# A two-dimensional Fourier mix and a gated expert: the Nyquist column broadcast by way of DRAM, and rows of x, fills and spills issued one transfer at a time

## The chip, the cores and the metric

The kernel runs on one core of a Trainium2 chip. The metric is the device time of one execution in microseconds. A core has five engines with programs of their own: TensorE (PE in the profile, its weight loads PEld), VectorE (DVE), ScalarE (ACT), GpSimd (POOL) and SyncE (SP), which here issues nearly all DMA transfers. All transfers of the core are carried by the same 16 DMA engines.

## The reference

All in float32. x has 8 batches of 3008 rows of 256 columns; w_in is 256 x 2048, w_out 2048 x 256.

```python
X = np.fft.fft(x, axis=1)          # over the 3008 rows
X = np.fft.fft(X, axis=2).real     # over the 256 columns
h = X.reshape(24064, 256) @ w_in
g = h * (1.0 / (1.0 + np.exp(-1.702 * h)))
out = g @ w_out
```

## The kernel before

**The transform.** 3008 is 47 x 64. Rows are viewed as 47 groups of 64; `fold1` and `mix1` do the length-47 part with matrices in `w1` on the tile `xt` (slots folded in pairs on POOL, then matmuls, then ACT copies back into `xt`). `spill` writes `xt` to the DRAM tensor `Td[b]`, `fill` reads it back in another layout into the tile `t4`, `rotate` corrects one column of it with a small matmul, and `stage2` does the length-64 part for a third of the rows, transposing the results on VectorE into the tile `pq`. Before a batch can be folded, `turn` writes the rows of x in reversed order into the DRAM tensor `Xr[b]` (three transfers), and `load_x` loads the forward and reversed rows into `xt` (four pieces of two transfers).

**The columns.** The transform over the 256 columns is folded into the weights: `wcs` holds w_in multiplied by cosines and sines. Since a real transform is symmetric, only half of the columns is stored; column 128 (the Nyquist column) takes the place of an unused part and is one row, partition 0 of `pq[:, 1]`, of 512 values. `nyquist` makes a tile `nb` of it in which all 128 partitions hold that row. ScalarE's `middle` (L566) multiplies `nb` by one factor a partition and writes the product into the PSUM bank x, to which the matmuls of `begin` (L495) then add the rest of the hidden layer.

**The expert.** The main loop goes over steps `(b, blk, hh, p)`: 8 batches, 3 blocks of `pq` a batch, 2 halves, 8 pairs of 128 hidden units: 384 steps. A step makes the hidden values of one pair for 2 x 256 outputs: sigmoid-gated forward values (L578) and, by the symmetry, backward values (L539, L581). From step 8 on the second product uses a Strassen-like scheme: `sums` and `deeper` form sums and differences on POOL and VectorE (L588 to L625), and the matmuls of `product` (L495) and `small_products` (L659) use seven products for eight, some of them twice nested. Products of step t run with step t + 3. At the end of each group of eight steps the result is combined, transposed into the tile `os` and stored by `store` (L799), in groups of four transfers.

**The order.** No scheduler reorders anything: the instructions of each engine stand in the order in which the Python code emits them. Work other than the steps' own hangs on slots: `at(t, fn, ...)` appends a function to slot t, and it is emitted at the end of step t. For batch b with t0 = 48 b, slots t0 + 6 on hold the folds and mixes of batch b + 1, then its spill, fill and rotate, and the turn and load of batch b + 2; slots t0 + 8, t0 + 24 and t0 + 40 hold the `stage2` of the next block, the slots after these its `nyquist`. In the first batch folds to loads come five slots later (`late`) and rotate three. A slot orders instructions on each engine and sets no time: an engine runs on until a semaphore holds it. SyncE's transfers take eight completion semaphores in turn, so an issue also waits for the transfer eight before it. `nb` and `pq` have two buffers, `xt` and `t4` one.

The very first block's `nyquist` is made by a matmul with a row of ones instead, and batch 0 is loaded and mixed by functions of its own ahead of the loop; neither is touched.

Of the kernel before, what the change touches and what calls it, by code (L numbers as in the profile page):

```python
# [27 lines left out]
F32 = mybir.dt.float32  # L28
# [6 lines left out]
NA, NB = 47, 64  # L35
NJ = NB // 2
NM = 48
ENDS = 0, NJ, NJ + 1, NJ + 2
PIECES = (0, 32), (32, NA)
# [7 lines left out]
def view(ap, offset, *dims):  # L47
    return bass.AP(ap.tensor, ap.offset + offset, [list(d) for d in dims])


def free(ap, offset, *dims):
    return bass.AP(ap.tensor, ap.offset + offset, [list(ap.ap[0])] + [list(d) for d in dims])
# [59 lines left out]
def kernel(ctx: ExitStack, tc, x, w_in, w_out, tab1, tab2, out):  # L112
    nc = tc.nc
    B, S, D = x.shape
    DF = w_in.shape[1]
    H = D // 2
    NF = DF // 128
    NBLK = NG // 4
# [10 lines left out]
    ctx.enter_context(tc.manual_schedule())  # L129

    Xr = [nc.dram_tensor(f"Xr{b}", (NA, NJ, D), F32, kind="Internal").ap() for b in range(B)]
    Td = [nc.dram_tensor(f"Td{b}", (NG * 128, D), F32, kind="Internal").ap() for b in range(B)]

    w1 = const.tile([128, (NJ + 3) * NM + 64 - NM], F32, tag="w1", name="w1")
# [31 lines left out]
    def bank(name, tag=None):  # L166
        if tag is None:
            tag = spare.pop(0)
            spare.append(tag)
        if tag in ("o0", "o1"):  # L170
            return o_banks[int(tag[1])]
        return (rest if tag[0] == "o" else psp).tile([128, 512], F32, tag=tag, name=name)
# [5 lines left out]
    t4t, pqt, nbt = {}, {}, {}  # L178
    xt = xp.tile([128, NJ, D], F32, tag="x", name="xt")

    def turn(b):

        for m0, m1 in ((NJ + 1, NJ + 17), (NJ + 17, NB)):
            n = m1 - m0
            nc.sync.dma_start(out=view(Xr[b], (m0 - NJ - 1) * D, [D, n], [NJ * D, NA], [1, D]),
                              in_=view(x[b], ((NA - 1) * NB + m0) * D, [D, n], [-NB * D, NA], [1, D]))
        nc.sync.dma_start(out=Xr[b][:, NJ - 1, :], in_=x[b].rearrange("(p j) d -> p j d", j=NB)[:, NJ, :])

    def load_x(b):

        for r in range(2):
            for p0, p1 in PIECES:
                t, src = xt[64 * r + p0:64 * r + p1], x[b].rearrange("(p j) d -> p j d", j=NB)[p0:p1]
                pairs = [4 * D, 8], [1, 2 * D]
                for lo, rows_, at in ((0, src, 2 * r), (16, Xr[b][p0:p1], 2 - 2 * r)):
                    nc.sync.dma_start(out=t[:, lo:lo + 16, :].rearrange("p (i c) d -> p i (c d)", c=2),
                                      in_=free(rows_, at * D, *pairs))

    e0 = {}

# [115 lines left out]
        for _ in range(n):  # L316
            nc.tensor.matmul(ps[:], lhsT=wcs[0][:, 0:128], rhs=wcs[0][:, 0:512], start=True, stop=True)

    def spill(b):

        for c in range(2):
            nc.sync.dma_start(out=view(Td[b], 16 * c * D, [NJ * D, NM], [1, 16 * D]),
                              in_=xt[64 * c:64 * c + NM, 0:16, :].rearrange("p q d -> p (q d)"))

    def fill(b, a0=0, a1=NG):
        if a0 == 0:
# [30 lines left out]
    def nyquist(b, blk):  # L357

        nb = nbt[b, blk] = pqp.tile([128, 512], F32, tag="nb", name="nb")
        row = pqt[b, blk][0:1, 1, :]  # L360
        if (b, blk) != (0, 0):
            nc.sync.dma_start(out=nb[:], in_=free(row, 0, [0, 128], [1, 512]))
            return
        ps = bank("psn")
        nc.tensor.matmul(ps[:], lhsT=ones[:], rhs=row, start=True, stop=True)
        nc.scalar.copy(nb[:], ps[:])


    raw = {}

# [457 lines left out]
    for e in odds:  # L828
# [7 lines left out]
                      in_=view(tab1, 0, [tab1.shape[1], 128], [28 * NM, 2], [1, ends]))  # L836
# [70 lines left out]
    def at(t, fn, *args):  # L907
        extra.setdefault(t, []).append((fn, args))

    n = len(steps)  # L910
# [9 lines left out]
        at(t, load_out, c, nc.sync)  # L920
    at(3, load_matrices)
    if B > 1:
        at(3, turn, 1)
        at(3, load_x, 1)
    at(4, rotate, 0, 4, NG)
    for i in range(NCK):
        at(7 + i, differences, i)
# [1 line left out]
    for b in range(B):  # L929
        t0 = b * NBLK * NF  # L930
        late = 0 if b else 5
        if b + 2 < B:
            at(t0 + 10, turn, b + 2)
        if b + 1 < B:
            for c in range(NCH):
                for part in range(2):
                    at(t0 + 6 + 2 * c + part + late, fold1, b + 1, c, part, nc.gpsimd)
                if c % 2:
                    at(t0 + 9 + 2 * c + late, mix1, b + 1, c // 2)
            at(t0 + 24 + late, spill, b + 1)  # L940
            at(t0 + 29 + late, fill, b + 1)
            if b + 2 < B:
                at(t0 + 33 + late, load_x, b + 2)
            at(t0 + 36 + 3 * (late > 0), rotate, b + 1)
        for blk in range(NBLK):
            nxt = (b, blk + 1) if blk + 1 < NBLK else (b + 1, 0)
            if nxt[0] < B:
                at(t0 + blk * NF + 8, stage2, *nxt)
                at(t0 + blk * NF + 9, nyquist, *nxt)

    for t in range(n + LAG):
        if t < NP:
# [7 lines left out]
            if t == 0:  # L960
                low_up(in2)
                nyquist(0, 0)
                low_down(in2)
# [94 lines left out]
```

## Time and profile before

| | us |
|---|---|
| median of 5 runs (lowest, highest) | 1876.4 (1874.68, 1877.94) |
| the profiled execution, device time | 1875.33 |
| its span in the profile | 1873.3 |
| ACT busy, L566 alone | 1149.7, 352.8 |
| SyncE's waits at L799 for the transposes into os | 1256.2 |
| issue of an nb broadcast on SyncE (median of 23) | 0.545 |
| DMA: bytes moved, mean rate | 105.21 MB, 56 GB/s |

The span is the time from the first to the last instruction in one profiled execution; the device time of that execution holds some 2 us more. Busy time is the time in which an engine had an instruction under way; issuing a transfer is not counted as busy. In a row of waits stand the engine and line that waited, what released it, and the total in us, the number of times and the longest. "Issue" as the releaser means that the engine waited for nothing that the profile shows.

### The profile page before, as it was taken

What the parts mean: (1) busy time and instruction counts of PE and PEld (TensorE: products, weight loads), DVE (VectorE), ACT (ScalarE), POOL (GpSimd) and SP (SyncE); (2) the same over time, 40 slices, a digit from 0 to 9 for tenths busy, and PEclk for the clock granted to TensorE, in tenths of its full rate; (3) what the DMA queues carried; (4) which work ended last, traced back from release to release, by engine and by line L of the source; (5) the groups of instructions that cost most, each with busy time, mean ns of one, the idle gap of its engine ahead of it and who ended that gap; (6) DMA issues with size and microseconds to landing.
All of it is one profiled execution on the core that took longest, in us unless ns stands there. A gap on an engine that the chain in (4) does not pass through costs nothing.

```text
span 1873.3 us, 55597 instructions
## 1 busy us (share of the span) xinstructions
PE 1851.7 (99%) x23600; PEld 1413.3 (75%) x23600; DVE 1532.1 (82%) x2245; ACT 1149.7 (61%) x2248; POOL 964.2 (51%) x1058
## 2 busy tenths in 40 slices
PE   9999999999999999999999999999999999999998
PEld 6577778777777777777777777777778777778776
DVE  7788878888789877988788878888788888878874
ACT  6655655666566656666565666656666656656663
POOL 4577345744367443673347733485435754434442
PEclk9999999999999999999999999999999999999999
DMA  8732351336221362305513164042631231312211
GB/s 283 172 52 17 80 90 19 51 51 118 24 18 47 53 121 19 52 17 97 77 15 52 23 117 53 13 63 46 111 25 25 19 51 47 29 15 17 20 22 23
DMA packets 145415, 105.21 MB, mean 56 GB/s; under 512 B 104914, under 2 KB 127986, under 8 KB 143984
## 3 DMA queue, kind: packets, MB, share of 16 engines
q1 hardware_dynamic: 143952, 101.14, 32.6%
q8 instruction: 186, 3.05, 0.7%
q10 hardware_dynamic: 1216, 0.52, 0.1%
q14 instruction: 61, 0.50, 0.1%
HBM read 58.38 MB, written 48.01 MB: 57 GB/s over the span
## 4 chain that ended last, share of the span: by engine, by line
PE 89%; DVE 5%; ACT 3%; DMA 1%; issue 1%; POOL 1%; SPq 0%; DVEq 0%; ACTq 0%; POOLq 0%
PE x L495 33%; PE o L495 25%; PE low L659 23%; PE o L659 4%; DVE big L625 2%; PE ps L348 1%; PE ps L246 1%; DVE big L762 1%; DVE big L539 1%; ACT x L566 1%; DMA big<-in_moe_w_in_dram 1%; PE psw L461 1%; ACT xt L249 1%; ACT big L581 0%; DVE big L671 0%
## 5 line engine op out<-in xcount | busy, mean ns | idle before, releaser
L596 POOL TENSOR_TENSOR big<-big 128x256 f32<-128x256 f32 (+1 forms) x376 | 349.9, 931 | 846.1 <-ACT big L588 716.3
L495 PE MATMUL x<-pq,wcs 128*64 128x256 f32 (+1 forms) x6016 | 777.6, 377 | 6.1 <-ACT x L566 3.1
L625 DVE TENSOR_TENSOR big<-big 128x512 f32<-128x512 f32 (+1 forms) x736 | 640.8, 885 | 30.8 <-PE low L659 14.3
L495 PE MATMUL o<-big,wo 128*64 128x256 f32 (+1 forms) x4800 | 627.1, 375 | 0.4 <-DVE big L603 0.4
L495 PEld LDWEIGHTS x<-pq,wcs 128*64 128x64 f32 x6016 | 415.6, 137 | 195.3 <-issue 14.6
L495 PEld LDWEIGHTS o<-big,wo 128*64 128x64 f32 x4800 | 345.5, 137 | 147.6 <-DVE big L603 1.2
L578 ACT ACTIVATE g<-x 128x512 f32<-128x512 f32 (+1 forms) x376 | 221.8, 590 | 374.9 <-PE x L495 373.8
L539 DVE TENSOR_TENSOR big<-g,x 128x512 f32<-128x512 f32 (+2 forms) x440 | 254.2, 589 | 202.8 <-ACT big L581 202.2
L659 PE MATMUL low<-big 128*64 128x128 f32 (+1 forms) x5888 | 385.1, 270 | 1.4 <-issue 1.4
L659 PEld LDWEIGHTS low<-big 128*64 128x64 f32 x5888 | 340.3, 137 | 29.7 <-issue 1.6
L566 ACT ACTIVATE x<-nb,af 128x256 f32<-128x256 f32 (+1 forms) x752 | 352.8, 469 | 12.2
L597 POOL TENSOR_TENSOR big<-big 128x256 f32<-128x256 f32 (+1 forms) x376 | 359.0, 955 | 0.0
L581 ACT ACTIVATE big<-x 128x512 f32<-128x512 f32 (+1 forms) x376 | 220.5, 586 | 201.3 <-PE x L495 185.4
L588 ACT ACTIVATE big<-big 128x512 f32<-128x512 f32 (+1 forms) x376 | 231.8, 616 | 44.9 <-DVE big L539 43.6
L659 PE MATMUL low<-big,wo 128*64 128x128 f32 (+1 forms) x2944 | 223.3, 271 | 0.1
L659 PEld LDWEIGHTS low<-big,wo 128*64 128x64 f32 x2944 | 174.9, 137 | 3.6 <-DVE big L625 0.4
L604 DVE TENSOR_TENSOR big<-big 128x512 f32<-128x512 f32 (+1 forms) x188 | 149.6, 796 | 6.5
L603 DVE TENSOR_TENSOR big<-big 128x512 f32<-128x512 f32 (+1 forms) x188 | 137.3, 730 | 4.7 <-POOL big L596 4.7
L659 PEld LDWEIGHTS o<-big,wo 128*64 128x64 f32 x1472 | 94.0, 137 | 24.6 <-issue 0.2
L762 DVE TENSOR_TENSOR big<-big,low 128x512 f32<-128x512 f32 (+3 forms) x184 | 109.1, 610 | 3.5
L659 PE MATMUL o<-big,wo 128*64 128x128 f32 (+1 forms) x1472 | 111.8, 271 | 0.0
L218 POOL TENSOR_TENSOR xt<-xt 111x510 f32<-111x510 f32 x56 | 77.2, 1379 | 4.4
(103 smaller groups left out, 975.2 us busy)
## 6 DMA issues: line engine op xcount, KB each, us to landing
out_dram<-os SPq DMA_DIRECT2D x284, 64.0 KB
Td<-xt SPq DMA_DIRECT2D x14, 768.0 KB
t<-Td SPq DMA_DIRECT2D x7, 1536.0 KB
xt<-in_x_dram SPq DMA_DIRECT2D x14, 512.0 KB
xt<-Xr SPq DMA_DIRECT2D x14, 512.0 KB
nb<-pq SPq DMA_DIRECT2D x23, 256.0 KB
out_dram<-os SPq DMA_DIRECT2D x96, 56.0 KB
Xr<-in_x_dram SPq DMA_DIRECT2D x7, 752.0 KB
```

What stands on the lines that cost most here:

```text
L495: nc.tensor.matmul(out[c0:c0 + 64], lhsT=lhs[:, c0:c0 + 64], rhs=rhs, skip_group_check=True, **how)
L539: nc.vector.tensor_tensor(free(out, at + m - 1, [by, 2], [RUN, blocks], [-1, m]), *ins, op=op)
L566: nc.scalar.activation(x[:, i * 256:i * 256 + n], nbt[b, blk][:, hh * 256:hh * 256 + n], ACTF.Copy, scale=af1[:, f:f + 1])
L578: nc.scalar.activation(two(g[:], n), two(xb[t][:], n), ACTF.Copy, scale=2.0)
L581: nc.scalar.activation(front(t), two(xb[t][:], width(t)), ACTF.Gelu_apprx_sigmoid)
L588: nc.scalar.activation(back(t), back(t), ACTF.Gelu_apprx_sigmoid)
L596: eng.tensor_tensor(right(t, S1, n), left(t, A21, n), right(t, A22, n), op=ALU.add)
L597: eng.tensor_tensor(left(t, S3, n), left(t, A11, n), left(t, A21, n), op=ALU.subtract)
L603: eng.tensor_tensor(s2, s1, a11, op=ALU.subtract)
L604: eng.tensor_tensor(s4, a12, s2, op=ALU.subtract)
L625: nc.vector.tensor_tensor(out, i0, i1, op=how)
L659: nc.tensor.matmul(o, lhsT=lhs, rhs=rhs, start=first_in, stop=(p == NP - 2), skip_group_check=True)
```

## The change

The row that `nyquist` spreads over the partitions is first written to a new DRAM tensor `Nd`, one row a block (`nyquist_out`, in the slot where `nyquist` stood), and `nyquist`, one slot later, reads that row from DRAM with a step of 0 over the partitions. `turn`, `load_x` and `spill` take an index and issue one piece a call; they are put into consecutive or alternating slots. `fill` is called for each block's four sections in slots of their own.

```diff
--- before.py
+++ after.py
@@ -129,6 +129,7 @@
     ctx.enter_context(tc.manual_schedule())
 
     Xr = [nc.dram_tensor(f"Xr{b}", (NA, NJ, D), F32, kind="Internal").ap() for b in range(B)]
+    Nd = nc.dram_tensor("Nd", (B * NBLK, 512), F32, kind="Internal").ap()
     Td = [nc.dram_tensor(f"Td{b}", (NG * 128, D), F32, kind="Internal").ap() for b in range(B)]
 
     w1 = const.tile([128, (NJ + 3) * NM + 64 - NM], F32, tag="w1", name="w1")
@@ -178,23 +179,24 @@
     t4t, pqt, nbt = {}, {}, {}
     xt = xp.tile([128, NJ, D], F32, tag="x", name="xt")
 
-    def turn(b):
-
-        for m0, m1 in ((NJ + 1, NJ + 17), (NJ + 17, NB)):
-            n = m1 - m0
-            nc.sync.dma_start(out=view(Xr[b], (m0 - NJ - 1) * D, [D, n], [NJ * D, NA], [1, D]),
-                              in_=view(x[b], ((NA - 1) * NB + m0) * D, [D, n], [-NB * D, NA], [1, D]))
-        nc.sync.dma_start(out=Xr[b][:, NJ - 1, :], in_=x[b].rearrange("(p j) d -> p j d", j=NB)[:, NJ, :])
-
-    def load_x(b):
-
-        for r in range(2):
-            for p0, p1 in PIECES:
-                t, src = xt[64 * r + p0:64 * r + p1], x[b].rearrange("(p j) d -> p j d", j=NB)[p0:p1]
-                pairs = [4 * D, 8], [1, 2 * D]
-                for lo, rows_, at in ((0, src, 2 * r), (16, Xr[b][p0:p1], 2 - 2 * r)):
-                    nc.sync.dma_start(out=t[:, lo:lo + 16, :].rearrange("p (i c) d -> p i (c d)", c=2),
-                                      in_=free(rows_, at * D, *pairs))
+    def turn(b, k):
+
+        if k == 2:
+            nc.sync.dma_start(out=Xr[b][:, NJ - 1, :], in_=x[b].rearrange("(p j) d -> p j d", j=NB)[:, NJ, :])
+            return
+        m0, m1 = ((NJ + 1, NJ + 17), (NJ + 17, NB))[k]
+        n = m1 - m0
+        nc.sync.dma_start(out=view(Xr[b], (m0 - NJ - 1) * D, [D, n], [NJ * D, NA], [1, D]),
+                          in_=view(x[b], ((NA - 1) * NB + m0) * D, [D, n], [-NB * D, NA], [1, D]))
+
+    def load_x(b, k):
+
+        r, (p0, p1) = k // 2, PIECES[k % 2]
+        t, src = xt[64 * r + p0:64 * r + p1], x[b].rearrange("(p j) d -> p j d", j=NB)[p0:p1]
+        pairs = [4 * D, 8], [1, 2 * D]
+        for lo, rows_, at in ((0, src, 2 * r), (16, Xr[b][p0:p1], 2 - 2 * r)):
+            nc.sync.dma_start(out=t[:, lo:lo + 16, :].rearrange("p (i c) d -> p i (c d)", c=2),
+                              in_=free(rows_, at * D, *pairs))
 
     e0 = {}
 
@@ -316,11 +318,10 @@
         for _ in range(n):
             nc.tensor.matmul(ps[:], lhsT=wcs[0][:, 0:128], rhs=wcs[0][:, 0:512], start=True, stop=True)
 
-    def spill(b):
-
-        for c in range(2):
-            nc.sync.dma_start(out=view(Td[b], 16 * c * D, [NJ * D, NM], [1, 16 * D]),
-                              in_=xt[64 * c:64 * c + NM, 0:16, :].rearrange("p q d -> p (q d)"))
+    def spill(b, c):
+
+        nc.sync.dma_start(out=view(Td[b], 16 * c * D, [NJ * D, NM], [1, 16 * D]),
+                          in_=xt[64 * c:64 * c + NM, 0:16, :].rearrange("p q d -> p (q d)"))
 
     def fill(b, a0=0, a1=NG):
         if a0 == 0:
@@ -359,12 +360,16 @@
         nb = nbt[b, blk] = pqp.tile([128, 512], F32, tag="nb", name="nb")
         row = pqt[b, blk][0:1, 1, :]
         if (b, blk) != (0, 0):
-            nc.sync.dma_start(out=nb[:], in_=free(row, 0, [0, 128], [1, 512]))
+            nc.sync.dma_start(out=nb[:], in_=view(Nd, (b * NBLK + blk) * 512, [0, 128], [1, 512]))
             return
         ps = bank("psn")
         nc.tensor.matmul(ps[:], lhsT=ones[:], rhs=row, start=True, stop=True)
         nc.scalar.copy(nb[:], ps[:])
 
+
+    def nyquist_out(b, blk):
+        i = b * NBLK + blk
+        nc.sync.dma_start(out=Nd[i:i + 1, :], in_=pqt[b, blk][0:1, 1, :])
 
     raw = {}
 
@@ -920,8 +925,10 @@
         at(t, load_out, c, nc.sync)
     at(3, load_matrices)
     if B > 1:
-        at(3, turn, 1)
-        at(3, load_x, 1)
+        for k in range(3):
+            at(3, turn, 1, k)
+        for k in range(4):
+            at(3, load_x, 1, k)
     at(4, rotate, 0, 4, NG)
     for i in range(NCK):
         at(7 + i, differences, i)
@@ -930,23 +937,28 @@
         t0 = b * NBLK * NF
         late = 0 if b else 5
         if b + 2 < B:
-            at(t0 + 10, turn, b + 2)
+            for k in range(3):
+                at(t0 + 11 + k, turn, b + 2, k)
         if b + 1 < B:
             for c in range(NCH):
                 for part in range(2):
                     at(t0 + 6 + 2 * c + part + late, fold1, b + 1, c, part, nc.gpsimd)
                 if c % 2:
                     at(t0 + 9 + 2 * c + late, mix1, b + 1, c // 2)
-            at(t0 + 24 + late, spill, b + 1)
-            at(t0 + 29 + late, fill, b + 1)
+            for c in range(2):
+                at(t0 + 24 + c + late, spill, b + 1, c)
+            for blk in range(NBLK):
+                at(t0 + 28 + blk + late, fill, b + 1, 4 * blk, 4 * blk + 4)
             if b + 2 < B:
-                at(t0 + 33 + late, load_x, b + 2)
+                for k in range(4):
+                    at(t0 + 32 + 2 * k + late, load_x, b + 2, k)
             at(t0 + 36 + 3 * (late > 0), rotate, b + 1)
         for blk in range(NBLK):
             nxt = (b, blk + 1) if blk + 1 < NBLK else (b + 1, 0)
             if nxt[0] < B:
                 at(t0 + blk * NF + 8, stage2, *nxt)
-                at(t0 + blk * NF + 9, nyquist, *nxt)
+                at(t0 + blk * NF + 9, nyquist_out, *nxt)
+                at(t0 + blk * NF + 10, nyquist, *nxt)
 
     for t in range(n + LAG):
         if t < NP:
```

## The prediction, made before the changed kernel ran

> **What bounds the kernel now.** I read the page's head and busy table first, then the waits of TensorE and of its weight loads, then the spacing of the steps, then the stretches around the two longest late waits, with SyncE's timeline and the DMA packets.
>
> ```profile
> span 1873.3 us, 55597 instructions
> PE 1851.7 (99%) x23600; PEld 1413.3 (75%) x23600; DVE 1532.1 (82%) x2245; ACT 1149.7 (61%) x2248; POOL 964.2 (51%) x1058
> q1 hardware_dynamic: 143952, 101.14, 32.6%
> q8 instruction: 186, 3.05, 0.7%
> ```
>
> TensorE is busy for 99% of the span. The steps repeat: from one back-half sigmoid (L581) to the next, the same slot takes the same time in batches 1 to 6 to within 0.02 us with few exceptions (4.77 us in slot 32, 4.33 in slot 33), and a batch of 48 slots takes 225.7 us (4.70 a slot). So no wait that recurs in every batch is waiting for a transfer, and a gain can come only from irregular holes. The longest waits of TensorE's matmuls:
>
> ```profile
> PE x L495 <- ACT x L566: 3.1, 5, 2.2
> ...
> PE ps L246 <- issue: 1.5, 1, 1.5
> PE low L659 <- issue: 1.4, 1, 1.4
> ```
>
> The 2.2 us hole is at 106 us: L566 stood behind L588, and that behind VectorE's L539, at the end of a row of small weight differences. No transfer is in that chain. The other two have no releaser ("issue"): TensorE waited on nobody. One is at 259 us (chain of waits), one at 1016 us (TensorE's timeline):
>
> ```profile
> 258.10 1.08 PE low L659 x18
> 259.18 1.40 issue
> ```
> ```profile
> 1015.81 0.39 PE L246 MATMUL ps<-xt,w 47*64 47x256 f32 x3
> 1017.68 0.27 PE L246 MATMUL ps<-e,w 47*64 47x129 f32 x1 [1.48 <-issue]
> ```
>
> Both break a run of identical matmuls in the middle. What they share is a late instruction fetch. Queue q8 carries 186 packets of 16 KB; 47,695 matmuls and weight loads make 256 instructions a packet, so q8 is TensorE's own program. Its packets start 9.9 us apart in the median, but the one at 257.6 us came 17.0 us after its predecessor and took 1.4 us, and the one at 1015.0 came after 15.4 us and took 1.1. TensorE resumed about 1.5 us after each had landed. Around the second, SyncE had issued
>
> ```profile
> 1004.58 0.53 SPq L362 DMA_DIRECT2D nb<-pq  x1
> 1005.15 7.47 SPq L185 DMA_DIRECT2D Xr<-in_x_dram  x2
> ```
>
> and the stretches (PE, weight loads, DVE, ACT, POOL busy, clock, DMA share, GB/s) read
>
> ```profile
> 1005.00:1010.00 5.00, 5.00 (x66) 3.88 (x62) 4.10 (x8) 2.82 (x8) 3.50 (x5) 1.00 0.78 25
> 1010.00:1015.00 5.00, 5.00 (x78) 4.48 (x76) 4.83 (x9) 2.92 (x8) 4.22 (x5) 1.00 0.85 32
> 1015.00:1020.00 5.00, 3.52 (x44) 2.21 (x42) 3.82 (x6) 1.69 (x5) 3.81 (x4) 1.00 0.90 307
> ```
>
> The DMA engines are 80% busy and move 25 to 32 GB/s: that is the broadcast. Its 128 packets of 2 KB, all read from one partition of pq, take 1.084 us each (median), eight on each of 16 engines; from the first packet's start to the last one's end it is 9.5 us (1005.8 to 1015.4). The fetch starts as it drains. Six more fetches start within 0.6 us of the end of a broadcast (489, 789, 1168, 1394, 1468, 1693 us), late but not late enough to stop TensorE. The hole at 259 us lies in a load of x: eight transfers issued from 243.2 to 248.9 us, with 2 KB packets from 244 to 266 us.
>
> [...]
>
> **The change, part by part.**
>
> *The broadcast.* Removed: 23 transfers with 8 x 1.084 = 8.7 us of every DMA engine. Added: 23 rows pq to Nd and 23 broadcasts Nd to nb. The row is one partition's 2 KB: at most one packet of 1.1 us on one engine. A broadcast from DRAM isn't in the trace. The nearest row is the load of x, whose 2 KB packets take 0.084 us alone and 0.17 to 0.32 us in a crowd: 8 x 0.084 = 0.7 us to 8 x 0.32 = 2.6 us. All 128 read the same DRAM row, which the loads of x do not, so the upper end is open; I take 0.2 us, 1.6 us an engine, and keep 1.1 us (as slow as now) as the other end of no gain.
>
> *Its wait.* SyncE now waits for the row to land before it issues nb. Row: 1.3 us from issue to first packet (as 93.0 to 94.3 now), 1.1 us[...]. Consumer is L566 of slot 14; from the last packet to that L566 there are now 12.7 to 17.3 us in 22 of the 23 (the broadcast for (1, 0) is mixed with x packets and I could not separate it). So nb stays covered by five slots of TensorE work. The tightest is (0, 1): nb now follows twelve output stores, which end at 108.5 us; [...]the use is at 121.2. Cost 0[...]. Queued behind the waiting SyncE are the turns, and for some blocks a fill, a pair of x loads or stores; each has at least two slots in hand.
>
> *Issues.* 23 rows and 14 additional fills are 37 issues of some 0.5 us on SyncE, 18 us in all. SyncE waits 1256 us for VectorE's os, so this is hidden. The other four engines execute the same instructions in the same order; seven times the rotate matmul waits for three semaphores instead of one[...].
>
> *The spreading.* SyncE isn't clocked by slots: it runs ahead until something holds it, so only what stands between the pieces counts. First batch: the second spill goes behind four stores, the loads of x are cut by four stores and by one row and its broadcast. Other batches: the fill is cut in three by two groups of four stores, six of eight loads of x stay together and the last two go behind eight stores; two of three turns still follow nb directly, the small third follows four stores. So the 3 MB burst becomes one of about 2.5 MB. The last fill is issued with the stores of slot 30 and rotate comes at 36, six slots or 28 us for 0.5 MB; the last x pair has sixteen slots. Cost 0. In the first batch the burst that made the hole at 259 us is broken up; in later batches little is.
>
> *Sum*, on the profiled execution (1875.33 us with 2.0 us around its span): minus 1.48 for the hole at 1016, minus 1.40 for that at 259, minus some 0.4 for small irregularities (slot 41 of batch 4 0.28 us over the rest, slots 14 and 15 of batch 2 0.2): 1872.0 us. That run is 1.07 us under the median of 1876.4; the five runs, 1874.68 to 1877.94, differ by about one such hole, which fits fetches that miss by chance. With the holes gone the median falls to the same 1872.0, 4.4 us or 0.23% below. 0.2% (3.75 us) is about what a measurement of this kernel can tell from no change: from 1872.65 down it is faster, from 1880.15 up slower.
>
> **Rivals.**
>
> *One hole stays.* The load of x in later batches is still 2.5 MB at once; fetches at 675, 895 and 1355 us were already 5 to 8 us late there. For it: the pieces hardly part. Against: none of these stopped TensorE before. 1872.0 + 1.5 = 1873.5 us, no change.
>
> *Nothing moves.* The broadcast from DRAM is as slow as from one partition, or holes open elsewhere: other packets shift the phase of 186 fetches. 1876.4 us.
>
> *Slower: one DRAM row is worse than one partition.* If 128 reads of one row are served one after another at 1.5 us a packet, an engine is held for 12 us, more than the 9.9 us between fetches. A fetch then waits 0 to 12 us; taking that a wait over 7 us makes a hole, 5/12 of 23 broadcasts make holes of 2.5 us on average: 24 us, less 1.5, so 1899 us. It decides from about 1.2 us a packet, where the hold exceeds today's. For it: nothing in the trace reads one DRAM row in parallel. Against: x packets took 0.32 us at worst.
>
> **How the numbers follow.** All holes gone 0.55 (1871.0 to 1873.2, nine tenths of it under 1872.65); one stays 0.22; nothing moves 0.13; slower 0.10. Faster 0.50, no change 0.40, slower 0.10. The range from 1871.0 to 1877.0 leaves out the slow case and the edges.
>
> **What would show it.** Right: the nb broadcast gone from the DMA share (1.6 us at high GB/s where 9.5 us at 25 GB/s were), no "issue" wait above 1 us on TensorE after 100 us, q8 spacing below about 14 us, steps as before. Wrong: L566 waiting for nb, POOL's fold for x, the rotate matmul for t; broadcast packets over 1 us; holes of 1.5 us at other places.

## The result, and the profile after

The changed kernel takes 1872.72 us in the median (1871.38 to 1875.23, 20 runs), the kernel before 1876.53 in the same comparison (1874.68 to 1878.67, 38 runs): a ratio of 0.998, 95% interval 0.9974 to 0.9986, so 3.8 us or 0.20% faster. The profiled execution took 1871.72 us (1875.33 before).

The page after, the lines that answer to those of before:

```profile
span 1869.7 us, 55662 instructions
PE 1851.2 (99%) x23600; PEld 1413.0 (76%) x23600; DVE 1530.3 (82%) x2245; ACT 1149.1 (61%) x2248; POOL 963.7 (52%) x1058
q1 hardware_dynamic: 144222, 101.19, 25.0%
q8 instruction: 186, 3.05, 0.7%
```

No engine does less: TensorE's busy time went from 1851.7 to 1851.2 us, for the same 23,600 matmuls. What went is 3.6 us of span with nothing in it, and 7.6 points of the time in which the 16 DMA engines were held by queue q1 (32.6 to 25.0%), for the same 101 MB.

The longest waits of TensorE's matmuls after (total us, times, longest):

```profile
PE x L500 <- ACT x L571: 3.1, 5, 2.2
PE warm L319 <- DVE wcs L832: 2.6, 1, 2.6
PE x L500 <- ACT g L583: 2.4, 7, 0.4
PE psw L466 <- POOL wst L442: 1.6, 4, 0.5
```

L500, L571 and L586 are L495, L566 and L581 of before. The hole of 2.2 us at 106 us (a hole is a stretch in which TensorE stands still) is as it was. Both "issue" waits of before are gone, and no other stands there in their place. The step times, from one L586 to the next, say the same: slot 42 of batch 0 took 6.49 us before and 4.68 after, slot 11 of batch 4 7.36 and 5.60. The rest agree to a few hundredths, except for shifts of up to 0.3 us in slots 35 to 38 of batch 0, which cancel out, and 0.2 us less in slots 44 to 46 of batch 5 against slot 26 of batch 6, 4.98 us for 4.82. The two slots are nearly the whole difference: 1.81 + 1.76 = 3.57 us.

SyncE's timeline at the place where before issued a broadcast and two turns, and the stretches there (PE, weight loads, DVE, ACT, POOL busy, the granted clock of TensorE as a share of the full one, DMA share, GB/s):

```profile
1002.74 0.24 SPq L372 DMA_DIRECT2D Nd<-pq  x1
1003.91 0.35 SPq L363 DMA_DIRECT2D nb<-Nd  x1
1004.32 2.52 SPq L189 DMA_DIRECT2D Xr<-in_x_dram  x2
```
```profile
1000.00:1005.00 5.00, 5.00 (x116) 3.89 (x94) 5.00 (x10) 1.92 (x5) 3.94 (x5) 1.00 0.04 6
1005.00:1010.00 5.00, 5.00 (x68) 4.10 (x66) 4.07 (x7) 3.93 (x10) 4.49 (x6) 1.00 0.86 251
1010.00:1015.00 5.00, 5.00 (x72) 3.95 (x68) 4.83 (x11) 1.72 (x4) 3.56 (x5) 1.00 0.30 104
```

The row is written and awaited in 1.2 us, the broadcast and the turns follow, and the DMA engines are busy at 251 GB/s where they had been at 25. From first packet to last a broadcast takes 2.1 us (1.75 to 3.46; 9.6 before), with packets of 0.09 us in the median (1.081 before). The two turns after it are issued in 2.5 us in place of 7.5. What the new wait costs SyncE, from its own waits:

```profile
SPq L804 <- DVE os L718: 1243.9, 92, 49.0
SPq L372 <- DVE pq L355: 171.8, 23, 24.4
SPq L363 <- DMA Nd<-pq: 38.4, 22, 5.0
```

38.4 us in all, beside 1243.9 that it waits for VectorE anyway.

### The profile page after: what moved, and what is told of

The parts are those of the page before. It is cut to its first block, busy times and chain, and to the rows that moved or that the text cites. A ratio compares the mean times of both kernels' runs of the same rounds, so it can differ in the third digit from the quotient of the medians.

```text
span 1869.7 us, 55662 instructions
## 1 busy us (share of the span) xinstructions
PE 1851.2 (99%) x23600; PEld 1413.0 (76%) x23600; DVE 1530.3 (82%) x2245; ACT 1149.1 (61%) x2248; POOL 963.7 (52%) x1058
## 4 chain that ended last, share of the span: by engine, by line
PE 89%; DVE 6%; ACT 3%; DMA 1%; issue 1%; POOL 0%; SPq 0%; DVEq 0%; ACTq 0%; POOLq 0%
PE x L500 32%; PE o L500 25%; PE low L664 23%; PE o L664 4%; DVE big L630 2%; PE ps L349 1%; PE ps L248 1%; DVE big L767 1%; DVE big L544 1%; ACT x L571 1%; DMA big<-in_moe_w_in_dram 1%; PE psw L466 1%; ACT xt L251 0%; ACT big L586 0%; ACT g L583 0%
## 5 line engine op out<-in xcount | busy, mean ns | idle before, releaser
L500 PE MATMUL x<-pq,wcs 128*64 128x256 f32 (+1 forms) x6016 | 772.4, 377 | 6.1 <-ACT x L571 3.1
L500 PE MATMUL o<-big,wo 128*64 128x256 f32 (+1 forms) x4800 | 622.3, 375 | 0.4 <-DVE big L608 0.4
L500 PEld LDWEIGHTS x<-pq,wcs 128*64 128x64 f32 x6016 | 412.5, 137 | 195.1 <-issue 14.6
L500 PEld LDWEIGHTS o<-big,wo 128*64 128x64 f32 x4800 | 342.3, 137 | 147.0 <-DVE big L608 1.2
L571 ACT ACTIVATE x<-nb,af 128x256 f32<-128x256 f32 (+1 forms) x752 | 352.7, 469 | 12.2
L586 ACT ACTIVATE big<-x 128x512 f32<-128x512 f32 (+1 forms) x376 | 220.3, 586 | 199.9 <-PE x L500 180.9
```

The costliest lines, as they stand in the source:

```text
L500: nc.tensor.matmul(out[c0:c0 + 64], lhsT=lhs[:, c0:c0 + 64], rhs=rhs, skip_group_check=True, **how)
L571: nc.scalar.activation(x[:, i * 256:i * 256 + n], nbt[b, blk][:, hh * 256:hh * 256 + n], ACTF.Copy, scale=af1[:, f:f + 1])
L586: nc.scalar.activation(front(t), two(xb[t][:], width(t)), ACTF.Gelu_apprx_sigmoid)
```

## Experiments

Theory A: a transfer that holds the DMA engines for long delays TensorE's next 16 KB of instructions, and beyond its reserve TensorE runs dry. Theory B: the new order and spreading of transfers did it, and it does not matter where the broadcast reads from. Each time stands against that of the kernel before on the same chip. The diffs are cut to the lines that matter; `...` marks what is left out.

**Only the broadcast.**

```diff
...
-            nc.sync.dma_start(out=nb[:], in_=free(row, 0, [0, 128], [1, 512]))
+            nc.sync.dma_start(out=nb[:], in_=view(Nd, (b * NBLK + blk) * 512, [0, 128], [1, 512]))
...
-                at(t0 + blk * NF + 9, nyquist, *nxt)
+                at(t0 + blk * NF + 9, nyquist_out, *nxt)
+                at(t0 + blk * NF + 10, nyquist, *nxt)
```

> The kernel before with the row sent through DRAM alone; turns, loads, spills and fills stay in their old calls and slots. Theory A (a long broadcast holds the DMA engines, TensorE's next 16 KB of instructions come late, TensorE runs dry): the hole of the kind seen at 1016 us goes, that of the load of x at 259 us stays. About 1.8 us off, 1874.5 to 1875 us; broadcast packets about 0.1 us; no fetch starts as a broadcast ends; the longest issue wait of TensorE is one of about 1.4 us near 259 us. Theory B (the spreading and the new order of transfers do it, where the broadcast reads from doesn't matter): 1876.5 us, no change.

1873.96 us against 1876.63; ratio 0.9988 (0.9982 to 0.9995), half a microsecond better than expected. Batches 1 to 6 take 225.5 to 225.8 us each, so no hole at a broadcast. The one at the load of x stays, at 261 us, on the same small matmul:

```profile
PE low L664 <- issue: 1.1, 1, 1.1
```

**Only the spreading.** The changed kernel with the broadcast read straight from pq again, in slot 9 (the diff above, undone).

> The changed kernel with the broadcast again read straight from pq in slot 9, the spreading kept. Theory A: the hole near 259 us goes, broadcasts still hold the engines for 9.5 us, so one or two holes of 1.5 us remain at broadcasts: 1874 to 1875.5 us. Theory B: the whole gain, 1872.7 us.

1875.82 us against 1876.63; ratio 0.9995 (0.9987 to 1.0003), 0.3 us over the range of theory A and not told from no change by the time alone. The profile tells more: nothing near 259 us, and the hole at a broadcast again, 1016 us, on the first mix of the same block:

```profile
PE ps L248 <- issue: 1.4, 1, 1.4
```

Theory B, 1872.7 us, fails.

**Only the first load of x.** The kernel before, with the load for batch 2 alone in four slots:

```diff
...
-                at(t0 + 33 + late, load_x, b + 2)
+                for k in range(4 if late else 1):
+                    at(t0 + 37 + 2 * k if late else t0 + 33, load_x, b + 2, (k,) if late else range(4))
```

> The kernel before with one thing changed: the load of x for batch 2, issued in batch 0, in four slots as in the changed kernel. Broadcasts from pq, turns, spills, fills and the other loads stay. Theory A: this load alone makes the hole at 259 us, which the four kernels with the spreading lack and those without it have: 0.8 to 1.8 us off, 1874.6 to 1875.6 us, the hole at a broadcast may stay. Rival (the hole at 259 us goes because of the spills, fills or turns): 1876.4 us and a hole near 259.

1874.86 us against 1876.04; ratio 0.9992 (0.9984 to 1.0), at the edge of what the time can tell. The hole near 259 us is gone, that at a broadcast stays, at 1014.6 us:

```profile
PE ps L246 <- issue: 1.3, 1, 1.3
```

So of all that is spread, this load is what made that hole. The gains add up, as far as they are known (each to 1.2 to 1.5 us either way): 2.7 for the broadcast and 1.2 for this load, 3.9; the whole change gave 3.8. Of the twelve profiles of this study, the six that keep the burst in batch 0 (before, only the broadcast, both with quarters, both with a longer hold) have a hole without a releaser between 259 and 268 us, of over 1 us in five and 0.3 us in one; the other six have none there.

**The same source, cut in four.** Four broadcasts of 32 partitions from pq in place of the whole one, issued by ScalarE a slot apart:

```diff
...
-            nc.sync.dma_start(out=nb[:], in_=free(row, 0, [0, 128], [1, 512]))
...
+    def quarter(b, blk, q):
+        row = pqt[b, blk][0:1, 1, :]
+        nc.scalar.dma_start(out=nbt[b, blk][32 * q:32 * q + 32, :], in_=free(row, 0, [0, 32], [1, 512]))
...
+                for q in range(4):
+                    at(t0 + blk * NF + 9 + q, quarter, *nxt, q)
```

> The kernel before with the broadcast from pq cut into four of 32 partitions, issued by ScalarE in slots 9 to 12: the same source, the same 128 packets of 2 KB, but four holds of 2 x 1.08 us a slot apart in place of one of 9.5 us. Theory A: packets stay at 1.08 us and yet the fetches are no longer late at broadcasts: 1874.5 to 1875 us as with the row in DRAM alone, plus whatever 4 x 0.4 us of issues cost on ScalarE (61% busy; 0 to 3 us). Rival (reading one partition 128 times is what hurts TensorE, however it is cut): 1876.5 us or more, with holes at broadcasts.

1879.3 us against 1876.63; ratio 1.0015 (1.0008 to 1.0021): slower, outside what theory A gave. The step times show where: batches 1 to 6 take 225.5 us each, with no hole at any broadcast, but batch 0 takes 86.6 us from slot 8 to slot 24 in place of 80.9. There GpSimd's fold waited 9.5 us for a load of x, VectorE behind it 6.4, TensorE behind that 4.3:

```profile
POOL xt L216 <- DMA xt<-Xr: 9.5, 1, 9.5
DVE big L606 <- POOL big L599: 6.4, 1, 6.4
```

Why the first load was seen so late with ScalarE's transfers among SyncE's I did not find out. With that first broadcast left whole:

> As e3, but the first batch's broadcast for block 1 is left whole on SyncE. In e3's profile the batches 1 to 6 took 225.5 us each and no hole stood at a broadcast, but batch 0 lost 5.8 us up to slot 24, where GpSimd's fold waited 9.5 us for a load of x and VectorE behind it. Theory A: without that artefact 1873.5 to 1875 us, as with the row in DRAM alone, though every packet still takes 1.08 us from one partition. Rival (DRAM is needed, or ScalarE's issues cost the 5 us): 1877 us or more.

1873.73 us against 1876.43; ratio 0.9985 (0.9979 to 0.9992), as much as by way of DRAM. Its packets from pq still took 0.85 us in the median; a quarter held the engines for 2.4 us. The stretches at a broadcast:

```profile
1005.00:1010.00 5.00, 5.00 (x64) 3.88 (x62) 3.84 (x8) 2.87 (x8) 3.50 (x5) 1.00 0.18 13
1010.00:1015.00 5.00, 5.00 (x80) 4.50 (x78) 4.83 (x9) 2.91 (x8) 4.62 (x6) 1.00 0.49 20
1015.00:1020.00 5.00, 4.96 (x64) 3.42 (x61) 4.93 (x9) 3.39 (x8) 3.81 (x4) 1.00 0.26 13
```

The rate is poorer than before (13 to 20 GB/s, 25 to 32 before), the share of time at most 0.49 (0.78 to 0.85 before), and TensorE doesn't stop at a broadcast. What harmed was the length of one hold (9.6 us whole, 2.4 us a quarter), not reading one partition, and DRAM is one cure of two. The quarters also go by ScalarE's queue; this run does not separate that from the cutting.

**A longer hold.** The kernel before with a second broadcast of the row behind the first, into a scratch `Sc` in DRAM that nobody reads; then one of half the size; then the same second copy added to the changed kernel, from Nd.

```diff
...
             nc.sync.dma_start(out=nb[:], in_=free(row, 0, [0, 128], [1, 512]))
+            i = (b * NBLK + blk) * 128
+            nc.sync.dma_start(out=Sc[i:i + 128, :], in_=free(row, 0, [0, 128], [1, 512]))
```

> The kernel before with a second broadcast of the same row from pq, into a DRAM scratch that nobody reads, right behind the first: the hold becomes 17 to 19 us, longer than the 9.9 us between fetches. Theory A: nearly every one of 22 broadcasts makes at least one fetch 9 us late and a hole of 1.5 to 5 us: 1910 to 1985 us. Theory B and chance: nothing waits for the second copy, 1876 to 1878 us.

> As e4, but the second copy takes 64 partitions only: the hold becomes 9.5 + 4.3, about 14 us. Theory A: the cost grows with what a fetch waits beyond TensorE's reserve of some 7 us, so it lies between the kernel before (9.5 us: one or two holes) and e4 (+122 us at 19 us). With a fetch waiting 0 to 14 us and a hole for what exceeds 7 us, half of 23 broadcasts make 3.5 us each: 40 us, about 1915 us. Rival (the cost is per added byte or packet): half of e4's, 1937 us.

> The changed kernel with a second broadcast from Nd into a DRAM scratch that nobody reads, the counterpart of e4: as many added transfers and bytes as there, but with fast packets. Theory A: 256 KB at about 0.1 us a packet is a hold of 2 to 4 us more, shorter than TensorE's reserve: within 1.5 us of the changed kernel, 1872 to 1874.5 us. Rival (an added transfer of 256 KB per block costs time whatever its packets take): tens of us, as e4's 122.

| hold of a broadcast, us | kernel | us (before beside it) | ratio, interval |
|---|---|---|---|
| 9.6 | before | 1876.5 | |
| 14.5 | half more | 1896.36 (1876.04) | 1.0108, 1.0093 to 1.0123 |
| 19.3 | twice | 1998.58 (1876.63) | 1.0652, 1.0633 to 1.0672 |
| 2.1 and a second | changed, twice from DRAM | 1873.09 (1876.43) | 0.9981, 0.9974 to 0.9988 |

The waits of TensorE with twice the broadcast, one hole of it, and the stretches around that hole:

```profile
PE o L662 <- issue: 25.4, 4, 7.3
PE low L662 <- issue: 23.8, 6, 6.6
PE o L498 <- issue: 23.3, 4, 8.2
PE x L498 <- issue: 15.0, 5, 4.4
```
```profile
198.04 0.80 PE L662 MATMUL o<-big,wo 128*64 128x128 f32 x5 [6.34 <-issue]
```
```profile
180.00:185.00 5.00, 5.00 (x68) 3.92 (x64) 3.92 (x5) 3.53 (x8) 4.29 (x6) 1.00 0.89 27
185.00:190.00 5.00, 5.00 (x61) 3.73 (x58) 4.83 (x10) 3.12 (x6) 3.52 (x5) 1.00 0.87 26
190.00:195.00 5.00, 1.71 (x17) 1.01 (x14) 4.93 (x7) 3.12 (x6) 2.01 (x3) 0.97 0.91 27
195.00:200.00 5.00, 1.96 (x19) 1.96 (x20) 1.76 (x2) 0.00 (x0) 0.26 (x1) 0.50 0.20 14
```

No engine waited for the second copy, and yet it cost 122 us: 20 holes of over 1 us, 89 us together. The clock column shows the remainder: the granted clock falls to 0.50 while the hole still lasts and stays there for some us after it. Over the execution it was halved for 95.6 us (6.7 in that of before). 31 of these lie inside the holes and cost nothing more; the other 64 us at half speed are some 32 us, an estimate. The cost is not one per byte, since half the copy cost a sixth, 20 us; it comes where the hold passes TensorE's reserve, that is, the time for which it still ran when a packet of its instructions was late (in the kernel before it stopped at packets 8.3 and 8.4 us late, as the next section counts it). The two longest of the six holes over 0.9 us with half the copy, of 4.6 and 3.9 us, are both in the first line:

```profile
PE o L498 <- issue: 8.5, 2, 4.6
PE o L662 <- issue: 3.5, 2, 2.5
```

My formula for the half copy, 40 us, was twice too high (its reserve of 7 us was an estimate, from the packet that came 17.0 us after the one before it where 9.9 is the median), and the range for the whole too low, as it had left the clock out. The last row of the table is the control: as many transfers and bytes, fast packets, nothing lost that can be told from the changed kernel's 1872.7.

**Bursts truly parted.** The changed kernel with turns and loads put behind different groups of stores:

```diff
...
-                at(t0 + 11 + k, turn, b + 2, k)
+                at(t0 + (13, 21, 22)[k], turn, b + 2, k)
...
-                    at(t0 + 32 + 2 * k + late, load_x, b + 2, k)
+                    at(t0 + ((37, 38, 45, 46) if late else (31, 37, 38, 45))[k], load_x, b + 2, k)
```

> The changed kernel with the pieces put where stores really part them on SyncE: turns at t0 + 13, 21 and 22, loads of x at t0 + 31, 37, 38 and 45 (37, 38, 45 and 46 counted with the first batch's 5), so no burst of x is over about 1 MB. Theory A: the fetches that were still 5 to 8 us late at loads of x come in time, spacing of q8 below about 14 us; there was no hole left in the profile of the changed kernel, so 0 to 1.5 us off, 1871.3 to 1872.7 us. Rival (the spreading does nothing, only the broadcast counted): 1872.7 us, same.

1872.59 us against 1876.43; ratio 0.998 (0.9973 to 0.9987): the same as the changed kernel. After 100 us only 4 packets of q8 come over 14 us after the one before, in place of 8 (10 before), but with no hole left there is nothing to gain from it.

**The hole at 106 us.** The kernel of the last run, with the small weights in every second slot:

```diff
...
-        at(7 + i, differences, i)
-        at(8 + i, small_weights, i)
+        at(7 + 2 * i, differences, i)
+        at(8 + 2 * i, small_weights, i)
```

> e6 with the differences and small weights of the expert (POOL and VectorE, 4 pieces) in every second slot, 7 to 14, in place of 7 to 11. The 2.2 us hole of TensorE at 106 us is then due to VectorE's L539 standing behind small weights and not to a transfer: if so it shrinks, 1 to 3 us less than e6. Rival (the hole moves to the later slots, where POOL also folds): no change against e6.

1876.89 us against 1876.43; ratio 1.0005 (0.9998 to 1.0011), 4.3 us worse than the kernel it was made from. The hole moved and split, 3.6 us at 115 and 2.7 at 129, and it still waits for L571:

```profile
PE x L500 <- ACT x L571: 7.4, 6, 3.6
```

So it does depend on this work and not on a transfer, but spreading it is no cure.

## Why the prediction was right, point by point

**The cause** was right and is shown: holes without a releaser, at a broadcast and at a burst of x, from TensorE's instructions coming late. The length of the hold, varied from 2.1 to 19.3 us, turns them off and on; the two parts of the change, made one at a time, each remove their own hole. The traces also show it by a count. With TensorE's instructions numbered from its first, all 34 waits of its matmuls without a releaser (over 0.15 us) in the twelve profiles end at number 193 or 194 of a block of 256, and 256 instructions are one packet of q8. Each time as many packets had landed as such borders had been reached, the last of them 1.1 to 1.6 us earlier. So TensorE stood at the edge of a packet that had only just come.

**The reserve** is about one such block. In the kernel before, after its first 110 us, a packet starts 0.5 us (median) before TensorE enters the block ahead of the packet's own, and a block lasts 10 us in the median, 5.9 to 13.8. The packets behind the two holes started 8.4 and 8.3 us after that entry. A third, at 1394 us, started 8.2 us after it and made none; the others, and all of after, were at most 7.1 us late. Ahead of that stretch, at 103.8 us, one of before started 8.9 us after it, in a block of 15.8 us, and made none. The spacing of the packets, by which the prediction went, is a coarser sign, as blocks differ in length. Its list of fetches at the end of a broadcast, seven with that of the hole, was too short: of the 22 broadcasts that are not mixed with a load of x, 17 have a fetch starting within 0.6 us of their end. Its 47,695 instructions include 495 waits and drains beside the matmuls and weight loads.

**The sum** came out at 1872.0 us, and the profiled execution at 1871.7, but two terms were off against each other; that it came so close is luck. A hole was priced at its gap, 1.40 and 1.48 us; it lengthened its slot by 1.81 and 1.76. The gap counts from the end of the last matmul, which otherwise overlaps the next: from the start of one to the start of the other it is 1.67 and 1.86 us. The 0.4 us for small irregularities was wrong: slot 41 of batch 3 (the prediction has batch 4) took 4.93 us before and after, slots 14 and 15 of batch 2 also kept their times. They are not from late fetches at a broadcast.

**The median** is 1872.7, not 1872.0. It lies in the range given for all holes gone, 1871.0 to 1873.2, but at the border of 1872.65 drawn there between faster and no change; the interval of the ratio leaves 1 out. I had put the spread of the runs down to holes that miss by chance, so the median was to fall onto the profiled run. It did not: the runs after spread over 3.9 us, as those before over 4.0, and the median is again 1.0 us over the profiled one (1.2 before). For this reason the gain was 3.8 us and not 4.4. What makes that spread stays open, but the twelve profiles point to the start. The first L566, up to which all of them issue the same work, comes between 79.9 and 82.3 us; in the profiled executions before and after it came at 80.0, early in both. The stretch from slot 8 to slot 24 took 80.8 to 80.9 us in eight. Each of these has after the hole at 106 us either a spell of half the granted clock, 3.4 us long, or a second hole of 2.0 us; two others (only the spreading, half a copy more) have both, and 82.2 us.

**The broadcast from DRAM** was priced at 1.6 us an engine, with an open upper end because all 128 packets read one row. From first to last packet it was 2.1 us, so the rival in which one DRAM row is worse than one partition fell.

**The wait for the row.** How long a row takes to land was not shown by the trace of before. After, the timeline has 1.2 us in the median from the issue of the row to that of nb (14.1 for block 1 of batch 0, with twelve stores between), and the last packet of a broadcast comes 3.1 us after its issue in the median: together some 4 us after the first issue, where it came 10.8 us after it before (1004.6 to 1015.4). For block 1 of batch 0 it came at 111.5 us, and the use at 121.2. L571 is seen waiting for nb nowhere.

**The spreading** went as read from the order on SyncE: late fetches persist at later loads of x; after 100 us eight packets are over 14 us apart, the largest spacing 18.5. The sign I gave, under 14 us, did not come true; it was too strict, since none of them stops TensorE. Breaking the first batch's burst was worth the one hole, as counted. The 37 more issues cost nothing that the profile shows, and the seven added semaphore waits of the rotate matmul (nine at L335 after, two at L334 before) are 51 ns each, with no gap of TensorE's matmuls there.

## What to carry to other kernels

When the bounding engine stops in the middle of a run of identical instructions and the profile names no releaser, look at what held the DMA engines just before. Here TensorE's instructions came as transfers too, 186 packets of 16 KB, and the packets behind the two holes started 15.4 and 17.0 us after the one before them (9.9 in the median). What counted was the time for which one burst held the engines, not its bytes: 256 KB in 9.6 us made a hole, 256 KB in 2.1 us made none, nor did the same twice over. So look for many microseconds of a high DMA share, be it at a low rate (25 to 32 GB/s in the broadcast) or a high one (135 to 193 GB/s in the load of x), and shorten it, by a faster source or by cutting it into pieces that something really parts. Here several transfers in a row on one queue remained one burst, whatever slots they were written for: the two turns behind a broadcast were still issued within 2.5 us.

## What the runs showed of the hardware

- 128 packets of 2 KB from one SBUF partition took 1.08 us each; the same row from one DRAM row, read 128 times over, 0.09 us in the median.
- TensorE's instructions came in packets of 16 KB, 256 instructions each, and its waits for them, 34 in twelve profiles, all ended at the edge of a packet. In the kernel before, TensorE stopped at the two packets that started 8.3 and 8.4 us after it had entered the block ahead of theirs, and did not at two that started 8.2 and 8.9 us after it; in the changed kernel the latest came 7.1 us after and made no hole. A hold of 9.6 us made one hole in 23 broadcasts; with one of 19.3 us the whole run had 20 holes over 1 us.
- Some holes had a further price, a spell at half the granted clock. In the kernel before, the hole of 2.2 us that began at 106.2 us was followed by 3.4 us at 0.50, from 108.8 us on; with twice the broadcast the clock was 0.50 from 195 to 200 us, at the hole of 6.3 us that ended at 198.0, and 0.976 in the mean of the run. In the twelve profiles every hole of 3.4 us and more after the first 100 us came with a spell at a granted clock of 0.50, of 3.4 to 10.2 us, which began 2.1 to 5.0 us after the hole did. Of the holes of 2.0 to 2.9 us some were followed by 3.4 us of it and some were not; those under 2.0 us were not, the two that the change removed, of 1.4 and 1.5 us, among them.
